# One run of key-value products per batch, and straight query pairs in the first two batches

## The chip, the cores and the metric

The kernel runs on one core of a Trainium2 chip. The metric is the device time of one execution in microseconds (us). Five engines work side by side, each in its own program order: TensorE multiplies matrices, VectorE does arithmetic between tensors, ScalarE functions and copies, GpSimd reductions over partitions, and SyncE issues the transfers (DMAs). Engines wait for each other by semaphores only.

## The reference

It is a linear attention, followed by a feed-forward layer with a gelu. For each of 8 batches and 8 heads (sequence 576, head size 64):

```
q_s = softmax of q over the 64 features
k_s = softmax of k over the 576 positions
kv  = k_s^T @ v               # 64 x 64 per head
x   = q_s @ kv                # 576 x 64 per head, heads side by side: 4608 x 512
h   = x @ w_in                # 512 x 2048
out = (h * sigmoid(1.702 h)) @ w_out
```

All is float32. The two weight matrices arrive as 64-bit floats and are turned into a high and a low 32-bit part in the kernel.

## The kernel before

**Tiles.** The 4608 tokens are 12 tiles (`t`) of 384, three to a partition. A batch is 576 tokens, one tile and a half: batch 0 starts at tile 0, batch 1 in tile 1, batches 2 to 7 in tiles 3, 4, 6, 7, 9, 10. Heads are taken in four pairs (`hp`). For a new batch, the keys' softmax numerators are made (`k_max`, `k_sub`: VectorE, GpSimd, and ScalarE for the exponential), then `kv_pair` (L435) multiplies keys by values: for each of a pair's two heads four full matmuls and one for the 64 positions left over ("tail"), with a column of ones in the values, whose product is the softmax's sum. TensorE runs each of these matmuls as two passes, so a pair shows as 20 in the trace, 64 columns wide, the two heads in two halves of the array. VectorE takes the reciprocal of the sum (L460, L461) and ScalarE scales the two 64x64 results into `kvn` (L466). Then queries are normalized (`q_soft`), transposed on TensorE (`q_tr`, L516) and multiplied with `kvn` (`x_pairs`): with one pair in a call as one 128x128 product whose off-blocks are zeros (L559), with two pairs as four 64x64 products that share the array (L564).

**Turned pairs.** For the four products of L564 to lie on different parts of the array, every second pair is held turned: its two heads change places, in the query's buffer (by the order of loading) and in `kvn`. This is done for all batches, though in tiles 0 and 1 the calls take one pair each.

**Feed-forward.** For each tile, 16 steps (`j`): `g1` (L589, 12 matmuls), gelu, and two steps later `g2` (L621, 9 matmuls). The first two tiles run interleaved, while the weights of the 16 steps are loaded (`load_w`, L218 and L223) and converted (`conv_w`: L248, L261 on ScalarE, L252, L256, L257, L267 on VectorE). The attention of a later tile is spread among the feed-forward steps of the tiles before it.

**Buffers and loads.** Batches 0 and 1 load all four heads of a group at once into memory that weights take over later. From batch 2 on keys and values go pair by pair through two buffers each (`kt_`, `vt_`): pairs 2 and 3 can be loaded only when the products of pairs 0 and 1 have read theirs. All loads are issued by SyncE, in one queue: `load_k` (L314, L319), `load_tail` (L298, L301), `load_v` (L330, one per head), `load_q` (L363 for tile 0, L368 else), with rows of 64 floats.

**Order.** A planner (`Plan`, L18) holds all operations with an engine, a cost, the buffers they read and write, and a rank, the due time. It runs a small model of the engines, always starting the ready operation of lowest rank, and the kernel's program on each engine is that order. So an operation's rank and cost say where it comes; on the chip the order is fixed. The rank of a task of tile t is `n0(i)`, i sixteenths of the way from three steps after the last step of tile t - 2 to the first step of tile t, 14 steps in all. Before, pairs 0 to 3 had their products at 4, 5.5, 10 and 11.5 and the query products of pairs 0 and 1 at 7.5, of pairs 2 and 3 at 13.5.

Of the kernel before, what the change touches and what calls it, by code (L numbers as in the profile page):

```python
# [107 lines left out]
def efficient_attention_then_gelu_ffn(  # L108
# [13 lines left out]
    nc = tc.nc  # L122
    B, H, S, D = q.shape
    NTOK, DM = out.shape
    FF = w_out.shape[0]
    P = 128
# [3 lines left out]
    NP = H // 2  # L130
# [4 lines left out]
    CM = SM // P  # L135
    ST = S - SM
    W = D + 1
# [4 lines left out]
    plan = Plan()  # L142

    bank = [psum.tile([P, 512], F32, name=f"bank{i}") for i in range(8)]

    def sb(name, shape, dtype=F32, tag=None):
        return const.tile(shape, dtype, name=name, tag=tag or name)

    ident = sb("ident", [P, P])
    kvn = [sb(f"kvn{i}", [P, NP, P]) for i in range(2)]  # L150
# [1 line left out]
    g = [sb(f"g{i}", [P, TB]) for i in range(3)]  # L152
    gs = [[sb(f"g{s}{i}", [P, TB], F32R) for s in "hl"] for i in range(LAG + 1)]
    tmp = [sb(f"tmp{i}", [P, DM]) for i in range(3)]
    kt_ = [sb(f"kt{i}", [P, CM, 2, D]) for i in range(2)]
    vt_ = [sb(f"vt{i}", [P, 2, CM, W]) for i in range(2)]
    qTs = [sb(f"qT{i}", [P, TB]) for i in range(2)]
    qt_ = [sb(f"qt{i}", [P, C, 2, D]) for i in range(2)]
    mx_ = [sb(f"mx{i}", [P, 4, D]) for i in range(2)]
# [26 lines left out]
    ek, em, ev, eq, en, etail = {}, {}, {}, {}, {}, {}  # L186
# [97 lines left out]
    def group(b):  # L284
        return 4 if b < 2 else 2

    kbuf, vbuf, qbuf, tbuf = {}, {}, {}, {}
# [17 lines left out]

    def load_k(b, i, rank):
        n = group(b)
        t, key = ek[b, i] if b < 2 else (kt_[i % 2], ("kt", i % 2))
        kbuf[b, i] = t, key
        hs = slice(n * i, n * (i + 1))  # L310

        def run():
            if b == 0:
                nc.sync.dma_start(  # L314
                    out=t.rearrange("p h c d -> p h (c d)"),
                    in_=k[b, hs, 0:SM, :].rearrange("h (p c) d -> p h (c d)", c=CM),
                )
            else:
                nc.sync.dma_start(out=t, in_=k[b, hs, 0:SM, :].rearrange("h (p c) d -> p c h d", c=CM))  # L319

        plan.add("SP", plan.ISSUE, (), (key,), rank, run, size=n * SM * D * 4)

    def load_v(b, i, rank):
        n = group(b)
        t, key = ev[b, i] if b < 2 else (vt_[i % 2], ("vt", i % 2))
        vbuf[b, i] = t, key

        def run():
            for h in range(n):
                nc.sync.dma_start(  # L330
                    out=t[:, h, :, 0:D], in_=v[b, n * i + h, 0:SM, :].rearrange("(p c) d -> p c d", c=CM)
                )

        plan.add("SP", n * 0.6, (), (key,), rank, run, size=1.5 * n * SM * D * 4)

    def parts(t):

        t0 = t * TB
        b, s0 = divmod(t0, S)
        n = min(TB, S - s0)  # L340
        got = [(b, s0, 0, n // C)]
        if n < TB:
            got.append((b + 1, 0, n // C, P))
        return got

    def load_q(t, i, rank):
        n = group(t)
        qt, key = eq[t, i] if t < 2 else (qt_[i % 2], ("qt", i % 2))
        qbuf[t, i] = qt, key

        if t == 0:
            runs = [(0, 0, 2), (2, 3, 1), (3, 2, 1)]
        elif n == 4:
            runs = [(0, 0, 1), (1, 1, 1), (2, 3, 1), (3, 2, 1)]
        else:
            runs = [(0, 1, 1), (1, 0, 1)] if i % 2 else [(0, 0, 2)]

        def run():
            for b, s0, p0, p1 in parts(t):
                for o, h, m in runs:  # L360
                    src = q[b, n * i + h : n * i + h + m, s0 : s0 + (p1 - p0) * C, :]
                    if t == 0:
                        nc.sync.dma_start(  # L363
                            out=qt[p0:p1, o : o + m].rearrange("p h c d -> p h (c d)"),
                            in_=src.rearrange("h (p c) d -> p h (c d)", c=C),
                        )
                    else:
                        nc.sync.dma_start(  # L368
                            out=qt[p0:p1, :, o : o + m], in_=src.rearrange("h (p c) d -> p c h d", c=C)
                        )  # L370

        plan.add("SP", plan.ISSUE * len(parts(t)) * len(runs), (), (key,), rank, run, size=n * TB * D * 4)
# [57 lines left out]
    def next_bank(t):  # L430

        n = nb[t] = nb.get(t, -1) + 1
        return n % 6 if t == 0 else 3 * (t % 2) + n % 3

    def kv_pair(b, hp, t, rank):  # L435
        n = group(b)
        i, o = divmod(2 * hp, n)
        kt, key = kbuf[b, i]
        vt, vkey = vbuf[b, i]
        kl, vl, (lkey, vlkey) = tbuf[b]  # L440
        bk = next_bank(t)
        pk = bank[bk]
        w = 2 * W
        hs = slice(2 * hp, 2 * hp + 2)
        loc = slice(o, o + 2)
        dst = kvn[b % 2][:, hp, :]
        r = rs[hp % 2]

        def run():
            for c in range(CM + 1):  # L450
                for a in range(2):
                    lhs = kt[:, c, o + a, :] if c < CM else kl[:, 2 * hp + a, :]
                    rhs = vt[:, o + a, c, :] if c < CM else vl[:, 2 * hp + a, :]
                    r0 = (a ^ hp % 2) * D
                    nc.tensor.matmul(  # L455
                        pk[r0 : r0 + D, :W], lhs, rhs, start=c == 0, stop=c == CM, tile_position=(0, r0)
                    )

        def run_r():
            nc.vector.tensor_scalar_add(r, pk[:, D:W], 1e-9)  # L460
            nc.vector.reciprocal(r, r)  # L461

        def run_n():
            for a in range(2):
                rows, cols = (slice(x * D, (x + 1) * D) for x in (a ^ hp % 2, a))
                nc.scalar.mul(dst[rows, cols], pk[rows, 0:D], r[rows])  # L466

        PB, R, K = ("bank", bk), ("r", hp % 2), ("kvn", b % 2, hp)
        plan.add("PE", 1.15, (key, vkey, lkey, (lkey, i), vlkey), (PB,), rank, run)
        plan.add("DVE", 0.35, (PB,), (R,), rank, run_r)  # L470
        plan.add("ACT", 0.65, (PB, R), (K,), rank, run_n)

    rs = [sb(f"r{i}", [P, 1]) for i in range(2)]
    qm = [sb(f"qm{i}", [P, C, 4]) for i in range(2)]

    def q_soft(t, i, ranks):
# [166 lines left out]
    def step_rank(t, j):  # L643
        if t == 0:
            return 2 * j
        if t == 1:
            return 2 * j + JOIN
        return 2 * NJ + JOIN + (t - 2) * NJ + j

    def new_batch(t):  # L650

        return next((b for b, s0, *_ in parts(t) if s0 == 0), None)
# [3 lines left out]
    def at(rank, f, *a):  # L656
        tasks.append((rank, len(tasks), f, a))


    for i in range(2):  # L660
        at(-90 + i, load_k, 0, i)
        if i == 0:
            at(-89.5, load_tail, 0)
    for i in range(2):
        at(-88 + i, load_q, 0, i)
    for i in range(2):
        at(-86 + i, load_v, 0, i)
    for j in range(NJ):
        r = -84 if j < 1 else -70 + j
# [12 lines left out]
    def attend(t, b, r, step):  # L682
        for i in range(2):
            at(r, k_max, b, i)
            at(r + step, k_sub, b, i)
            at(r + step, lambda rank, t=t, i=i: q_soft(t, i, (rank, rank, rank)))
            for hp in (2 * i, 2 * i + 1):
                at(r + 3 * step, lambda rank, hp=hp: kv_pair(b, hp, t, rank))
                at(r + 3 * step, q_tr, t, hp)
                at(r + 3.5 * step, x_pairs, t, (hp,))  # L690
            r += 2 * step
# [5 lines left out]
    for j in range(NJ):  # L697
        r = -40 if j == 0 else 2 * j - 2.2
# [3 lines left out]
    for t in range(2, NB):  # L702
        end = step_rank(t, 0)
        start = step_rank(t - 2, NJ - 1) + 3
        b = new_batch(t)

        def n0(i):
            return start + i * (end - start) / NJ + 0.3

        for gq in range(2):  # L710
            i0 = 6 * gq
            for hp in (2 * gq, 2 * gq + 1):
                d = (hp % 2) * 1.5

                ld = n0(5 + d) + 0.1 if gq else n0(0) - (7 if t == 2 else 3) + d
                if b is not None:
                    if hp == 0:
                        at(ld, load_tail, b)
                    at(ld, load_k, b, hp)
                    at(ld + 0.1, load_v, b, hp)  # L720
                    at(n0(i0 + d), k_max, b, hp)
                    at(n0(i0 + 1 + d), k_sub, b, hp)
                    at(n0(i0 + 4 + d), lambda rank, b=b, hp=hp, t=t: kv_pair(b, hp, t, rank))
                at(ld + 0.2, load_q, t, hp)
                at(n0(i0 + 1 + d), lambda rank, t=t, hp=hp: q_soft(t, hp, (rank, rank, rank)))
                at(n0(i0 + 5 + d), q_tr, t, hp)
                if hp % 2:
                    at(n0(i0 + 6 + d), x_pairs, t, (hp - 1, hp))
    seq = sorted((step_rank(t, j), t, j) for t in range(NB) for j in range(NJ))
    for n, (r, t, j) in enumerate(seq):  # L730
# [35 lines left out]
```

## Time and profile before

| | us |
|---|---|
| median of 3 runs | 924.39 (924.11 to 924.57) |
| the profiled execution, its own time | 925.09 |
| its span, first to last instruction | 923.3 |

| engine | busy us | share | instructions |
|---|---|---|---|
| TensorE (PE) | 885.3 | 96% | 5048 |
| TensorE weight loads (PEld) | 778.6 | 84% | 5048 |
| VectorE (DVE) | 392.7 | 43% | 863 |
| ScalarE (ACT) | 499.6 | 54% | 848 |
| GpSimd (POOL) | 24.0 | 3% | 35 |

The mean granted clock of TensorE over the span was 0.988 of full speed (2.4 GHz; its other level is 1.2 GHz). Matmuls are pipelined: a row's time is one matmul's latency, so what TensorE's work costs is read from start to start, not from the sum of durations. SyncE's rows (SPq) are the issuing of transfers, not their movement. A line number stands for the line of the kernel that made the instruction.

### The profile page before, as it was taken

Reading aid. Unit: us, or ns where it says so; the run is one execution under the profiler, and the core shown is the slowest. Engines: PE = TensorE matmul, PEld = TensorE weight load, DVE = VectorE, ACT = ScalarE, POOL = GpSimd, SP = SyncE. Lnnn points to the kernel's source line nnn. Section 1 sums busy time; section 2 is a strip of 40 time slices with the busy share of each in tenths; the row PEclk is TensorE's granted clock in tenths of the full one; section 3 lists DMA queues with packets and bytes.
Section 4 is the critical chain, followed back from the end, with each engine's and each line's share of the span. In section 5 each row is a group of like instructions: output and inputs, shape, how many; then the busy total and the mean of one; then the engine's idle time right before and its main releaser. Section 6 shows DMA issues by size and latency. Waiting matters only on the chain.

```text
span 923.3 us, 12812 instructions
## 1 busy us (share of the span) xinstructions
PE 885.3 (96%) x5048; PEld 778.6 (84%) x5048; DVE 392.7 (43%) x863; ACT 499.6 (54%) x848; POOL 24.0 (3%) x35
## 2 busy tenths in 40 slices
PE   2669999999999999999999999999999999999998
PEld 2469989888888889889889889889888888988996
DVE  8789995173342451331542442322344243131111
ACT  3476666367573783552773765544467375252322
POOL 1000000000000000000000000000000000000000
PEclk9879999999999999999999999999999999999999
DMA  9799100121221220001230230000231110000000
GB/s 224 173 377 278 26 1 1 51 75 40 51 58 33 57 50 35 18 18 40 58 75 35 64 75 35 18 18 35 63 65 45 36 37 9 35 18 1 35 1 34
DMA packets 124795, 55.35 MB, mean 60 GB/s; under 512 B 107840, under 2 KB 118080, under 8 KB 124736
## 3 DMA queue, kind: packets, MB, share of 16 engines
q1 hardware_dynamic: 124736, 54.54, 22.6%
q8 instruction: 39, 0.64, 0.3%
q14 instruction: 20, 0.16, 0.1%
HBM read 45.09 MB, written 9.44 MB: 59 GB/s over the span
## 4 chain that ended last, share of the span: by engine, by line
PE 93%; SPq 3%; DMA 1%; DVE 0%; ACT 0%; issue 0%; ACTq 0%
PE bank L589 44%; PE bank L621 44%; PE bank L455 2%; PE bank L564 2%; PE bank L516 2%; SPq L368 1%; SPq L330 1%; DMA raw<-in_moe_w_in 1%; DMA eq<-in_q 1%; SPq L298 0%; PE bank L559 0%; SPq L319 0%; SPq L301 0%; SPq L218 0%; SPq L314 0%
## 5 line engine op out<-in xcount | busy, mean ns | idle before, releaser
L589 PE MATMUL bank<-xh,w 128*128 128x384 f32 x1536 | 431.5, 342 | 7.4 <-ACT w L261 7.4
L621 PE MATMUL bank<-w,gh 128*128 128x512 f32 x1152 | 365.6, 399 | 1.4 <-ACT gh L598 1.4
L589 PEld LDWEIGHTS bank<-xh,w 128*128 128x128 f32 x1536 | 283.2, 189 | 18.8 <-ACT w L261 7.6
L601 DVE TENSOR_TENSOR gl<-g,gh 128x384 fp32r<-128x384 f32 x192 | 107.0, 557 | 398.4 <-ACT gh L598 398.0
L595 ACT ACTIVATE g<-bank 128x384 f32<-128x384 f32 x192 | 94.3, 491 | 309.8 <-PE bank L589 309.1
L589 PE MATMUL bank<-xl,w 128*128 128x384 f32 x768 | 260.5, 339 | 0.0
L621 PEld LDWEIGHTS bank<-w,gh 128*128 128x128 f32 x1152 | 211.9, 189 | 43.1 <-issue 6.2
L621 PE MATMUL bank<-w,gl 128*128 128x512 f32 x576 | 228.3, 396 | 3.1 <-DVE gl L601 3.1
L589 PEld LDWEIGHTS bank<-xl,w 128*128 128x128 f32 x768 | 145.5, 189 | 6.5
L621 PEld LDWEIGHTS bank<-w,gl 128*128 128x128 f32 x576 | 108.7, 189 | 28.6 <-DVE gl L601 3.5
L598 ACT CAST gh<-g 128x384 fp32r<-128x384 f32 x192 | 98.6, 513 | 5.8
L595 ACT ACT_TABLE_LOAD x58 | 74.4, 1283 | 1.0
L489 DVE TENSOR_REDUCE qm<-qt 128x6 f32<-128x384 f32 x40 | 21.9, 548 | 51.4 <-DMA qt<-in_q 51.4
L493 ACT ACT_TABLE_LOAD x33 | 42.3, 1283 | 2.4 <-DMA qt<-in_q 1.8
L397 POOL PARTITION_ALL_REDUCE mx<-mx x28 | 22.9, 817 | 717.1 <-DVE mx L393 717.1
L523 ACT COPY qT<-bank 128x384 f32<-128x384 f32 x48 | 22.7, 475 | 26.6 <-PE bank L516 26.4
L466 ACT ACTIVATE kvn<-bank,r 64x64 f32<-64x64 f32 x64 | 19.7, 308 | 25.2 <-DVE r L461 23.1
L421 ACT ACT_TABLE_LOAD x25 | 32.1, 1283 | 1.2 <-PEq L753 0.7
L496 DVE TENSOR_REDUCE qm<-qt 128x6 f32<-128x384 f32 x40 | 22.0, 550 | 20.5 <-ACT qt L493 20.5
L248 ACT ACTIVATE tmp<-raw 128x512 f32<-128x512 f32 x32 | 21.5, 676 | 16.4 <-DMA raw<-in_moe_w_in 9.4
L534 DVE TENSOR_TENSOR xl<-bank,xh 128x384 fp32r<-128x384 f32 x48 | 24.7, 551 | 3.5 <-ACT xh L531 3.3
L490 DVE TENSOR_TENSOR qt<-qt,qm 128x384 f32<-128x384 f32 x40 | 22.3, 559 | 3.3
(72 smaller groups left out, 464.6 us busy)
## 6 DMA issues: line engine op xcount, KB each, us to landing
out<-tmp SPq DMA_DIRECT2D x36, 256.0 KB, 2.1
raw<-in_moe_w_in SPq DMA_DIRECT2D x16, 512.0 KB, 10.0
raw<-in_moe_w_out SPq DMA_DIRECT2D x16, 512.0 KB, 10.5
kt<-in_k SPq DMA_DIRECT2D x24, 256.0 KB, 3.5
vt<-in_v SPq DMA_DIRECT2D x48, 128.0 KB, 3.5
qt<-in_q SPq DMA_DIRECT2D x40, 96.0 KB, 2.8
qt<-in_q SPq DMA_DIRECT2D x14, 192.0 KB, 3.0
ek<-in_k SPq DMA_DIRECT2D x4, 512.0 KB, 6.4
```

Source lines behind the costliest of these rows:

```text
L397: nc.gpsimd.partition_all_reduce(flat, flat, P, bass_isa.ReduceOp.max)
L421: nc.scalar.activation(t, t, AF.Exp)
L490: nc.vector.tensor_tensor(out=qt, in0=qt, in1=bc(m, D), op=ALU.subtract)
L493: nc.scalar.activation(qt, qt, AF.Exp)
L496: nc.vector.tensor_reduce(out=m, in_=qt, axis=AX.X, op=ALU.add)
L523: nc.scalar.copy(qT, pq[:, :TB])
L534: nc.vector.tensor_tensor(out=xl, in0=px[:, :TB], in1=xh.bitcast(F32), op=ALU.subtract)
L589: nc.tensor.matmul(ph, wi[w][j][:, c, :], x[:, c, :], start=c == 0 and i == 0, stop=c == KC - 1 and i == 2,)
L595: nc.scalar.activation(gt, ph, AF.Gelu_apprx_sigmoid)
L598: nc.scalar.copy(gh, gt)
L601: nc.vector.tensor_tensor(out=gl, in0=gt, in1=gh.bitcast(F32), op=ALU.subtract)
L621: nc.tensor.matmul(po[c], x[:, cs], wo[w][j], start=j == 0 and i == 0, stop=j == NJ - 1 and i == 2)
```

## The change

It makes four edits. Keys and values get four buffers each in place of two, and a batch's four loads of each are asked for together before the tile's tasks. `kv_pairs` takes a list of pairs: from batch 2 on all four in one uninterrupted run on TensorE, into four stretches of one PSUM bank, due at 6.5; one addition and one reciprocal serve all four, and the eight scalings of ScalarE follow. In batches 0 and 1 it is called with one pair, as before. Pairs are turned only from batch 2 on, so the queries of tiles 0 to 2 are loaded straight, all heads of a group in one transfer per part; tile 2 (which belongs to batch 1) then calls `x_pairs` with single pairs. The planner's cost of the products goes from 1.15 a pair to 0.57 a pair and 0.36 a run, and that of the early query loads falls with the number of transfers.

```
-    kt_ = [sb(f"kt{i}", [P, CM, 2, D]) for i in range(2)]
-    vt_ = [sb(f"vt{i}", [P, 2, CM, W]) for i in range(2)]
+    kt_ = [sb(f"kt{i}", [P, CM, 2, D]) for i in range(NP)]
+    vt_ = [sb(f"vt{i}", [P, 2, CM, W]) for i in range(NP)]
...
+    def turned(b, hp):
+        return b > 1 and hp % 2 == 1
...
     def load_q(t, i, rank):
-        if t == 0:
-            runs = [(0, 0, 2), (2, 3, 1), (3, 2, 1)]
-        elif n == 4:
-            runs = [(0, 0, 1), (1, 1, 1), (2, 3, 1), (3, 2, 1)]
-        else:
-            runs = [(0, 1, 1), (1, 0, 1)] if i % 2 else [(0, 0, 2)]
+        runs = [(0, 1, 1), (1, 0, 1)] if turned(parts(t)[0][0], i) else [(0, 0, n)]
...
-    def kv_pair(b, hp, t, rank):
+    def kv_pairs(b, hps, t, rank):
...
+        pk = bank[bk][:, : len(hps) * W].rearrange("p (m w) -> p m w", w=W)
+        nr[0] += 1
+        r = rs[nr[0] % 2][:, : len(hps)]
...
         def run():
-            for c in range(CM + 1):
+            for m, hp in enumerate(hps):
+                i, o = divmod(2 * hp, n)
+                kt, vt = kbuf[b, i][0], vbuf[b, i][0]
+                for c in range(CM + 1):
+                    for a in range(2):
+                        lhs = kt[:, c, o + a, :] if c < CM else kl[:, 2 * hp + a, :]
+                        rhs = vt[:, o + a, c, :] if c < CM else vl[:, 2 * hp + a, :]
+                        r0 = (a ^ turned(b, hp)) * D
+                        nc.tensor.matmul(
+                            pk[r0 : r0 + D, m, :], lhs, rhs, start=c == 0, stop=c == CM, tile_position=(0, r0)
+                        )
...
+            nc.vector.tensor_scalar_add(r, pk[:, :, D], 1e-9)
+            nc.vector.reciprocal(r, r)
...
+        plan.add("PE", 0.57 * len(hps) + 0.36, reads, (PB,), rank, run)
+        plan.add("DVE", 0.35, (PB,), (R,), rank, run_r)
...
+                    nc.scalar.mul(kvn[b % 2][rows, hp, cols], pk[rows, m, 0:D], r[rows, m : m + 1])
...
-                    at(ld, load_k, b, hp)
-                    at(ld + 0.1, load_v, b, hp)
-                    at(n0(i0 + d), k_max, b, hp)
-                    at(n0(i0 + 1 + d), k_sub, b, hp)
-                    at(n0(i0 + 4 + d), lambda rank, b=b, hp=hp, t=t: kv_pair(b, hp, t, rank))
+                    lk = n0(0) - (7 if t == 2 else 3) + hp
+                    at(lk, load_k, b, hp)
+                    at(lk + 0.1, load_v, b, hp)
+                    at(n0(hp), k_max, b, hp)
+                    at(n0(hp + 1), k_sub, b, hp)
+                    if hp == NP - 1:
+                        at(n0(6.5), lambda rank, b=b, t=t: kv_pairs(b, range(NP), t, rank))
...
-                if hp % 2:
+                if t == 2:
+                    at(n0(i0 + 6 + d), x_pairs, t, (hp,))
+                elif hp % 2:
                     at(n0(i0 + 6 + d), x_pairs, t, (hp - 1, hp))
```

## Rows read from the trace of the kernel before

**Rows 1.** The page's line of engines: busy us (share of the span) x instructions.
```profile
PE 885.3 (96%) x5048; PEld 778.6 (84%) x5048; DVE 392.7 (43%) x863; ACT 499.6 (54%) x848; POOL 24.0 (3%) x35
```
**Rows 2.** Windows; PE, PEld, DVE, ACT, POOL busy; last: clock, DMA share, GB/s.
```profile
150.00:912.00 762.00, 762.00 (x4351) 670.46 (x4350) 261.03 (x608) 406.25 (x681) 16.83 (x23) 1.00 0.16 39
...
20.00:40.00 20.00, 14.85 (x95) 10.27 (x95) 18.45 (x35) 13.26 (x26) 2.12 (x2) 0.87 0.73 126
40.00:60.00 20.00, 9.52 (x78) 8.51 (x75) 12.09 (x24) 11.48 (x22) 0.00 (x0) 0.71 1.03 359
60.00:80.00 20.00, 19.09 (x110) 17.63 (x111) 18.30 (x36) 13.01 (x29) 0.00 (x0) 0.91 1.02 330
```
**Rows 3.** The chain that ended last, 0 to 90 us: start, us, what.
```profile
40.22 8.07 DMA raw<-in_moe_w_in
...
49.55 4.30 PE bank L589 x12
...
69.70 2.09 PE bank L589 x12
71.79 2.08 PE bank L621 x9
```
**Rows 4.** Timeline of SyncE, 0 to 110 us: start, us, issues merged by line.
```profile
3.34 3.26 SPq L363 DMA_DIRECT2D eq<-in_q  x6
...
20.15 13.45 SPq L368 DMA_DIRECT2D eq<-in_q  x16
33.65 5.32 SPq L330 DMA_DIRECT2D ev<-in_v  x8
39.01 0.62 SPq L218 DMA_DIRECT2D raw<-in_moe_w_in  x1
```
**Rows 5.** Windows of 2 us in the opening, columns as in rows 2.
```profile
24.00:26.00 2.00, 2.00 (x26) 1.28 (x26) 1.57 (x3) 1.93 (x6) 0.00 (x0) 1.00 1.14 168
...
28.00:30.00 2.00, 2.00 (x11) 1.69 (x11) 1.97 (x5) 1.35 (x4) 0.00 (x0) 1.00 0.35 80
```
**Rows 6.** The page's DMA issues: KB each, median us from issue to landing.
```profile
ev<-in_v SPq DMA_DIRECT2D x16, 128.0 KB, 3.3
...
eq<-in_q SPq DMA_DIRECT2D x16, 48.0 KB, 2.4
```
**Rows 7.** Timelines of VectorE and of ScalarE in the opening; idle before in brackets.
```profile
38.93 0.96 DVE L499 TENSOR_TENSOR eq<-eq,qm 128x768 f32<-128x768 f32 x1
45.54 0.43 DVE L252 TENSOR_SCALAR raw<-raw 128x512 uint32<-128x512 uint32 x1 [5.66 <-DMA raw<-in_moe_w_in]
...
54.52 0.48 ACT L523 COPY qT<-bank 128x384 f32<-128x384 f32 x1 [1.70 <-PE bank L516]
```
**Rows 8.** Line L455 from 150 us on: idle of its engine (us, times).
```profile
  issue: 6.2, 22
```
**Rows 9.** Timeline of TensorE around the first insertion of the third batch.
```profile
200.32 0.34 PE L589 MATMUL bank<-xh,w 128*128 128x384 f32 x1
200.59 0.69 PE L455 MATMUL bank<-vt,kt 128*64 128x65 f32 x16
201.10 0.29 PE L455 MATMUL bank<-vl,kl 128*64 128x65 f32 x4
...
201.60 0.33 PE L589 MATMUL bank<-xl,w 128*128 128x384 f32 x1
```
**Rows 10.** Instructions on the raw weights: ns min/median/max, first and last start us.
```profile
L248 ACT ACTIVATE tmp<-raw x32: 647/677/697, 17.9 to 133.4; 128x512 f32<-128x512 f32 x32
```
**Rows 11.** Timeline of TensorE: a paired insertion, then an unpaired one of tile 1.
```profile
182.95 0.34 PE L589 MATMUL bank<-xh,w 128*128 128x384 f32 x1
...
184.59 0.40 PE L621 MATMUL bank<-w,gl 128*128 128x512 f32 x1
...
67.28 0.39 PE L621 MATMUL bank<-w,gl 128*128 128x512 f32 x1
...
68.61 0.39 PE L621 MATMUL bank<-w,gl 128*128 128x512 f32 x1
```
**Rows 12.** The page's group of the scalings: busy, mean ns of one, idle before.
```profile
L466 ACT ACTIVATE kvn<-bank,r 64x64 f32<-64x64 f32 x64 | 19.7, 308 | 25.2 <-DVE r L461 23.1
```

More of the change, by code (lines that the diff above doesn't have):

```diff
@@ L307, in load_k @@
         n = group(b)
-        t, key = ek[b, i] if b < 2 else (kt_[i % 2], ("kt", i % 2))
+        t, key = ek[b, i] if b < 2 else (kt_[i], ("kt", i))
         kbuf[b, i] = t, key
@@ L324, in load_v @@
         n = group(b)
-        t, key = ev[b, i] if b < 2 else (vt_[i % 2], ("vt", i % 2))
+        t, key = ev[b, i] if b < 2 else (vt_[i], ("vt", i))
         vbuf[b, i] = t, key
@@ L363, in run @@
                         nc.sync.dma_start(
-                            out=qt[p0:p1, o : o + m].rearrange("p h c d -> p h (c d)"),
+                            out=qt[p0:p1].rearrange("p h c d -> p h (c d)"),
                             in_=src.rearrange("h (p c) d -> p h (c d)", c=C),
@@ L433, in next_bank @@
         return n % 6 if t == 0 else 3 * (t % 2) + n % 3
-    def kv_pair(b, hp, t, rank):
+    def kv_pairs(b, hps, t, rank):
         n = group(b)
-        i, o = divmod(2 * hp, n)
-        kt, key = kbuf[b, i]
-        vt, vkey = vbuf[b, i]
         kl, vl, (lkey, vlkey) = tbuf[b]
         bk = next_bank(t)
[L442 to L447, printed above, removed]
-        def run():
-            for c in range(CM + 1):
-                for a in range(2):
[L452 to L471, printed above, removed]
@@ L473, in efficient_attention_then_gelu_ffn @@
-    rs = [sb(f"r{i}", [P, 1]) for i in range(2)]
+        pk = bank[bk][:, : len(hps) * W].rearrange("p (m w) -> p m w", w=W)
+        nr[0] += 1
+        r = rs[nr[0] % 2][:, : len(hps)]
+        reads = [lkey, vlkey]
+        for hp in hps:
+            i = 2 * hp // n
+            reads += [kbuf[b, i][1], vbuf[b, i][1], (lkey, i)]
+        def run():
+            for m, hp in enumerate(hps):
[9 more added lines that the diff above has]
+                        )
@@ new lines, in run_r, with run_n @@
+        def run_r():
+            nc.vector.tensor_scalar_add(r, pk[:, :, D], 1e-9)
+            nc.vector.reciprocal(r, r)
+        PB, R = ("bank", bk), ("r", nr[0] % 2)
+        plan.add("PE", 0.57 * len(hps) + 0.36, reads, (PB,), rank, run)
+        plan.add("DVE", 0.35, (PB,), (R,), rank, run_r)
+        for m, hp in enumerate(hps):
+            def run_n(m=m, hp=hp):
+                for a in range(2):
+                    rows, cols = (slice(x * D, (x + 1) * D) for x in (a ^ turned(b, hp), a))
+                    nc.scalar.mul(kvn[b % 2][rows, hp, cols], pk[rows, m, 0:D], r[rows, m : m + 1])
+            plan.add("ACT", 0.65, (PB, R), (("kvn", b % 2, hp),), rank, run_n)
@@ L474, in efficient_attention_then_gelu_ffn @@
+    nr = [0]
+    rs = [sb(f"r{i}", [P, NP]) for i in range(2)]
     qm = [sb(f"qm{i}", [P, C, 4]) for i in range(2)]
@@ L687, in attend @@
             for hp in (2 * i, 2 * i + 1):
-                at(r + 3 * step, lambda rank, hp=hp: kv_pair(b, hp, t, rank))
+                at(r + 3 * step, lambda rank, hp=hp: kv_pairs(b, (hp,), t, rank))
                 at(r + 3 * step, q_tr, t, hp)
```

## The prediction

> **What bounds the kernel now.** The views, in the order of reading. The page's engine line first: TensorE is busy for 885.3 of 923.3 us [rows 1], so the reader looks for where it is not, and for what its busy time is spent on. The windows answer the first: from 150 to 912 us it is busy without a gap at the full 2.4 GHz, while from 20 to 40 us it is busy for 14.85 us and from 40 to 60 us for 9.52, at a mean granted clock of 0.71 [rows 2]. So there are two places to win: its own work in the long middle, and the opening. From 60 to 80 us it is busy for 19.09, with its last gap just after 60; a start of this dense part that comes n us earlier ends the kernel n us earlier, as long as the others keep up.
>
> The chain of waits tells what ends the opening's largest gap. It runs through a weight load issued at 40.22 that lands 8.07 us later, ScalarE's work on it, and the first product of the step at 49.55 [rows 3]. Going back, it is SyncE's own issuing: the sixteen query loads of the second token tile take SyncE 13.45 us from 20.15, the eight value loads behind them 5.32, and only then come the weights [rows 4]. Between 28 and 30 us the DMA engines are busy to 0.35 and move 80 GB/s, where between 24 and 26 they were full (1.14 at 168 GB/s) [rows 5]: past 26 us issuing is the limit, not moving.
>
> **Part 1, the query loads of the first two tiles.** Unturned, a group's four heads go in one transfer. The second tile's 16 issues become 4. SyncE's 13.45 us hold 16 issues, so one is at most 0.84; without the stall at their head it is about 0.65 (the eight value issues behind: 5.32/8 = 0.67) [rows 4]. Twelve fewer are 12 x 0.65 = 7.8 us, the most that the weights can move up. The first tile's 6 issues become 2, worth 4 x 0.54 = 2.2 us of 3.26 [rows 4], which I put at nothing: the DMA engines are full then and hide it (with that cover gone it would be 2.2 us more).
>
> The bytes do not shrink, so the engines bound it from below. At 26 us, where the engines first run dry, (26 - 20.15 - 3.05 of stall)/0.65, some 4 of the 16 query loads of 48 KB [rows 6] are through; 12 x 48 + 8 x 128 KB = 1.6 MB are left ahead of the weights. At 168 GB/s, the full rate of [rows 5], this takes 9.5 us and ends at 35.5; at 80/0.35 = 229 GB/s, 7.0 us and 33.0. Before, the last values were issued at about 38.3 and land 3.3 us later [rows 6], at 41.6. So the weights come 6.1 us earlier at least, and 7.8 at most (SyncE's own saving). A rule of the Trainium skill speaks for the lower end (DMA: Bandwidth & Descriptors, "Why small descriptors are slow"): each packet carries a fixed overhead whatever the issue, and 256-byte packets feel it. By it the bytes would go at the slower rate and the weights gain 6.1 us; the row of 0.35 shows that before, at least, the packets were not the limit.
>
> What is late next? VectorE: its last operation before the gap starts at 38.93 and takes 0.96, so it is free at 39.9, and it then stood idle 5.66 us until 45.54 for the weights [rows 7]. Weights that land 6.1 us earlier or more close this gap whole: 5.7 us, the lower end for the opening. TensorE's product could start near 43.5. The upper end is the clock. TensorE idles 7.39 us before 49.55 and its product then takes 4.30 us, against 2.09 at the full clock [rows 3]; ScalarE waits 1.70 us for TensorE at 54.52 because of it [rows 7]. With a gap of one or two us in place of 7.39 the clock may stay up, which gives up to 1.7 us more: 7.4. I take 6.8, since the gap almost vanishes. Behind it the weights' order is kept, and VectorE and TensorE move up together. (If VectorE moved up less than TensorE, TensorE would wait for it: that is the lower end, 5.7.)
>
> **Part 2, four products in one run.** From the third batch on (six batches), four separate insertions among the feed-forward products become one. There are 24 now, and 22 of them show an idle weight loader without any wait, 0.28 us each [rows 8]. One insertion in full [rows 9]: from the last ordinary start, 200.32, to the second ordinary start behind it, 201.60, are 1.28 us, where two ordinary spacings of 2.09/12 = 0.174 would be 0.35; it costs 0.93. The first sixteen of its 20 matmuls take 0.51 us from start to start, 0.032 each, so 20 carry 0.64, and 0.29 is spent going in and out. Three times less of that in six batches: 18 x 0.29 = 5.2 us. This is the lower end (the last four may start closer than the others; were they free, 0.42 would be in and out, 7.6 us). I take 0.30: 5.4 us. All of it is on the path, as TensorE is never idle there. The reciprocals drop from 4 to 1 pair of instructions a batch, on VectorE, which has slack: nothing. The keys and values of a batch are now requested together, two more of each kind at once; SyncE and the DMA engines (0.16 busy in the middle [rows 2]) hide that. At the start they stand before the last weights in SyncE's queue: 1 MB more, 4.5 to 6.0 us by the rates of part 1, hidden as long as they land before their conversions, the last of which starts at 133.4 [rows 10]. The two more fills of ones on VectorE lie in its idle start: nothing.
>
> **Part 3, the third tile's query products.** They lose the paired form: two insertions of four 64x64 products become four of one 128x128. Paired, an insertion costs 184.59 - 182.95 = 1.64, less one spacing of 0.17 and two of 2.08/9 = 0.23 [rows 3]: 1.01 us for two pairs. The second tile's unpaired form, two halves of 192 columns, costs 68.61 - 67.28 = 1.33, less three of 0.23: 0.64 for one pair [rows 11]. With 384 columns in one piece it has two passes in place of four, so at most 0.64 and at least two spacings and a way out, about 0.46. Four of these less two of the other: -0.2 to +0.5; I take +0.3. The Trainium skill (TensorEngine Tiling (Array Packing), "Theoretical Speedup") would have it dearer: work cut to 64x64 tiles may run up to four times faster, so untiling it should cost. By that rule, half the array now multiplies zeros and the time would double, +2.0 us; no row shows that.
>
> **Sum.** -6.8 - 5.4 + 0.3 = -11.9 us against the profiled execution's own 925.09 gives 913.2. That execution is 0.7 above the median of the three runs, 924.39; the prediction for the median is 912.5. A measurement of this kernel can tell about 0.2%, 1.85 us, from no change. Ends: -7.4 - 7.6 - 0.2 and -5.7 - 5.2 + 0.5 give 909.2 and 914.0.
>
> **Rivals.**
> Rival 1: the opening gains little, because the DMA engines stay full on small packets once they are issued faster, or VectorE takes its freed time for other work. Then only parts 2 and 3 count: 924.4 - 5.4 + 0.3 = 919.3, and with half the gain 915.9. Against it: busy shares of 0.35 in the stretch that matters [rows 5] and VectorE's 5.66 us of idleness for nothing but weights [rows 7].
> Rival 2: the merged run is followed too closely by its readers, and this ends slower. The first query products read the scaled results of ScalarE: eight scalings of 308 ns [rows 12] come now after the whole run, 2.5 us, where one pair's 0.6 did. The tasks stand 14/16 of a step apart, 0.875 x (2.09 + 2.08) = 3.6 us. If ScalarE is so late by its tables and gelus that all 2.5 us are waited for, six batches lose 15 us: 927.5. It decides from 2.0 us a batch, where the gain is gone. Against it: the order is made from costs of all engines, and today's has no wait of TensorE from 150 to 912 us [rows 2].
> Rival 3: the unpaired form streams its zeros at full price, so that the 1.01 us of each paired insertion doubles; part 3 then costs 2.0 us and not 0.3: 914.2. The second tile's 0.64 for a pair in the same form [rows 11] speaks against. (It is what the Trainium skill's page in part 3 would lead to.)
> Rival 4: the merged run gains nothing since its inner pairs pay the same way in and out: 917.9. Against: the in and out of [rows 9] lie between matmuls of different forms, and inside the run the form stays.
>
> **How the numbers follow.** Forecast 0.70 (909.2 to 914.0); rival 1 0.13, half of it below 917; rival 2 0.04; rival 3 0.06; rival 4 0.04; an order that the new costs shuffle, either way, 0.03. The range 908.5 to 917.0 holds the forecast, rival 3 and half of rival 1. Faster takes all but rival 2 and part of the shuffle: 0.94; same 0.02; slower 0.04.
>
> **What would show it.** Right: SyncE issues the first of the later weights near 31 us and not 39.01; VectorE has no gap of some 5 us near 40; the product of 49.55 starts near 43 and takes about 2.1 us; TensorE has six runs of 80 matmuls of about 2.85 us in place of 24 of 0.93; no waits behind them. Wrong: a DMA share near 1 from 26 us on with the weights still landing after 43 (rival 1), or TensorE waiting for the scalings behind a run (rival 2).

## The result, and the profile after

The median went from 924.28 us (924.11 to 924.57, four runs) to 915.93 (914.18 to 918.02, four runs): a ratio of 0.991, 95% interval 0.9884 to 0.9936, faster by 8.35 us. The forecast was 912.5 with a range of 908.5 to 917.0; its likeliest case alone reached to 914.0. The profiled execution took 914.53 us for a span of 912.8, where before's took 925.09 for 923.3.

Of the page of after, the line of engines and the group of the scalings (columns as in [rows 1] and [rows 12]):

```profile
PE 880.8 (96%) x5040; PEld 778.0 (85%) x5040; DVE 388.8 (43%) x829; ACT 494.1 (54%) x844; POOL 25.1 (3%) x35
...
L472 ACT ACTIVATE kvn<-bank,r 64x64 f32<-64x64 f32 x64 | 17.9, 306 | 14.1 <-DVE r L462 12.2
```

TensorE is again the bound. The scalings on ScalarE cost 306 ns each as before and wait for the reciprocals, but from 60 us on TensorE's products wait for nothing.

The windows of the opening (columns as in [rows 2]):

```profile
20.00:40.00 20.00, 14.63 (x98) 10.03 (x98) 18.32 (x36) 14.77 (x27) 2.13 (x2) 0.83 1.06 231
40.00:60.00 20.00, 14.60 (x126) 12.59 (x123) 18.65 (x38) 15.16 (x31) 0.00 (x0) 0.91 1.06 384
60.00:80.00 20.00, 19.89 (x100) 17.59 (x99) 19.35 (x35) 14.03 (x27) 0.00 (x0) 1.00 0.88 254
...
24.00:26.00 2.00, 1.94 (x28) 1.41 (x27) 1.93 (x6) 1.79 (x5) 0.00 (x0) 1.00 1.37 177
28.00:30.00 2.00, 2.00 (x11) 1.70 (x11) 1.97 (x5) 1.52 (x3) 0.00 (x0) 1.00 0.80 128
```

From 40 to 60 us TensorE is busy for 14.60 us, where it was 9.52, at a mean granted clock of 0.91 in place of 0.71 [rows 2]. From 28 to 30 us the DMA engines are busy to 0.80, where it was 0.35 [rows 5].

SyncE's timeline, then VectorE's and TensorE's where each begins on the second step (columns as in [rows 4] and [rows 7]):

```profile
3.33 1.35 SPq L362 DMA_DIRECT2D eq<-in_q  x2
4.72 7.81 SPq L330 DMA_DIRECT2D ev<-in_v  x8
...
19.90 4.93 SPq L367 DMA_DIRECT2D eq<-in_q  x4
24.88 7.37 SPq L330 DMA_DIRECT2D ev<-in_v  x8
32.29 0.62 SPq L218 DMA_DIRECT2D raw<-in_moe_w_in  x1
```

```profile
38.67 0.96 DVE L503 TENSOR_TENSOR eq<-eq,qm 128x768 f32<-128x768 f32 x1
39.55 0.42 DVE L252 TENSOR_SCALAR raw<-raw 128x512 uint32<-128x512 uint32 x1
```

```profile
42.95 0.44 PE L593 MATMUL bank<-xh,w 128*128 128x384 f32 x1 [1.65 <-ACT w L261]
```

The weights are issued at 32.29 in place of 39.01 [rows 4]. VectorE turns from the queries to the weights without a gap, where it stood idle 5.66 us [rows 7]. TensorE begins the step at 42.95 in place of 49.55 [rows 3], after 1.65 us of idleness and not 7.39.

TensorE around the run of the third batch (columns as in [rows 9]):

```profile
216.89 0.34 PE L593 MATMUL bank<-xh,w 128*128 128x384 f32 x1
217.06 0.49 PE L520 MATMUL bank<-ident,qt 128*128 128x128 f32 x3
217.48 0.69 PE L456 MATMUL bank<-vt,kt 128*64 128x65 f32 x16
218.00 0.29 PE L456 MATMUL bank<-vl,kl 128*64 128x65 f32 x4
218.11 0.64 PE L456 MATMUL bank<-vt,kt 128*64 128x65 f32 x16
218.58 0.29 PE L456 MATMUL bank<-vl,kl 128*64 128x65 f32 x4
218.70 0.64 PE L456 MATMUL bank<-vt,kt 128*64 128x65 f32 x16
...
219.75 0.29 PE L456 MATMUL bank<-vl,kl 128*64 128x65 f32 x4
219.97 0.74 PE L625 MATMUL bank<-w,gh 128*128 128x512 f32 x2
220.54 0.40 PE L625 MATMUL bank<-w,gl 128*128 128x512 f32 x1
```

The last ordinary start is 216.89, the second behind the run is one spacing of 0.23 before 220.54, at 220.31: 3.42 us, less spacings of 0.17 and 0.23, is 3.01. The three transposes of a query tile, which stand in the same gap, cost 0.33 in such a gap alone. The run costs 2.69 us, against 4 x 0.93 [rows 9], and there are six: 6 x 1.03 = 6.2 us saved. The view of the line's idle time from 150 us on counts the ways in, 22 before [rows 8]:

```profile
  issue: 1.0, 6
```

The third tile's query products, two pairs one behind the other (same view as the run):

```profile
175.32 0.33 PE L593 MATMUL bank<-xh,w 128*128 128x384 f32 x1
175.50 1.45 PE L563 MATMUL bank<-qT,kvn 128*128 128x384 f32 x4
176.49 0.92 PE L625 MATMUL bank<-w,gh 128*128 128x512 f32 x2
177.25 0.39 PE L625 MATMUL bank<-w,gl 128*128 128x512 f32 x1
```

Worked in the same way these two pairs cost 1.28 us, the other two, which stand behind transposes, 1.48: together 2.76, where the paired form took 2 x 1.01 [rows 11]. The loss is 0.75 us.

**Where the time went.** A step that no part but the opening touches yet starts at 172.04 us before and at 164.32 after: the opening gives 7.7. From there to the end before takes 751.3 us and after 748.5, only 2.8 less, where the run (6.2) less the third tile (0.75) should give 5.4. So 2.6 us are lost somewhere in the middle, in which TensorE's products never wait. The ordinary products show it: counted over all steps that nothing interrupts, twelve products of the first weights take 2104 ns from start to start before and 2109.5 after, three of the second weights 695.3 and 698.6.

### The profile page after: what moved, and what is told of

It is laid out like the page before. It is cut to its first block, busy times and chain, and to the rows that moved or that the text cites. A ratio compares the mean times of both kernels' runs of the same rounds, so it can differ in the third digit from the quotient of the medians.

```text
span 912.8 us, 12680 instructions
## 1 busy us (share of the span) xinstructions
PE 880.8 (96%) x5040; PEld 778.0 (85%) x5040; DVE 388.8 (43%) x829; ACT 494.1 (54%) x844; POOL 25.1 (3%) x35
## 4 chain that ended last, share of the span: by engine, by line
PE 94%; DVE 4%; ACT 1%; DMA 1%; issue 0%; SPq 0%; ACTq 0%; DVEq 0%
PE bank L593 44%; PE bank L625 44%; PE bank L456 2%; PE bank L520 2%; PE bank L568 2%; PE bank L563 1%; DMA ek<-in_k 1%; DVE eq L494 0%; DVE tmp L257 0%; DVE tmp L256 0%; DVE qm L493 0%; DVE qm L500 0%; DVE w L267 0%; DVE em L414 0%; DVE xl L538 0%
```

## The experiments

**Is it the chip, and do the parts add up?** Four kernels on one chip, five rounds each; before and after again, and each part by itself. The before of this chip is 925.16.

> The kernel before once more, on the chip of the three runs below. Theory A (the ordinary feed-forward products became slower by the change: three g2 products took 695 ns from start to start in the trace of before and 698.6 in that of after, twelve g1 products 2103 and 2109): the same 695 and 2103 here. Rival B (that difference is one of chips or of days): 698 to 699 and 2109 here, and the time of before about 3 us longer than 924.3.

> The changed kernel once more, with more runs. Its four runs lay at 914.2 to 914.5 and at 917.3 to 918.0. Theory: two courses of the opening, told apart by how long TensorE's clock is at half (10.2 us in the trace at hand, one stretch of 3.4 us more in the longer runs), so the runs fall into the same two groups and the trace shows the group of its own time. Rival: a spread without groups, from the transfers. Theory A: g2 products at 698.6 ns again. Rival B: whatever the kernel before shows on this chip.

e1 gave 924.68 (ratio 0.9997, 0.9989 to 1.0006), e2 916.59 (0.9902, 0.9887 to 0.9918). The ordinary products of e1 take 695.4 and 2103.5 ns, those of e2 698.6 and 2109.5: the slower pace goes with the kernel, not with the chip.

The query loads and the third tile alone, with two buffers and four separate products a batch:

```
+    def turned(b, hp):
+        return b > 1 and hp % 2 == 1
-        if t == 0:
-            runs = [(0, 0, 2), (2, 3, 1), (3, 2, 1)]
...
+        runs = [(0, 1, 1), (1, 0, 1)] if turned(parts(t)[0][0], i) else [(0, 0, n)]
...
-                    r0 = (a ^ hp % 2) * D
+                    r0 = (a ^ turned(b, hp)) * D
...
+                if t == 2:
+                    at(n0(i0 + 6 + d), x_pairs, t, (hp,))
```

> The straight query pairs of batches 0 and 1 alone, with separate products and two buffers. Additive theory: the opening's 7.5 us less and the third tile's 0.8 more, so 917.6; TensorE's product of the second step starts at 43 and not at 49.5. Rival: the opening needs the earlier keys as well, and less than 4 us come: over 920. If the slower ordinary products come from the larger buffers, they are at 695 ns here.

920.4 us, ratio 0.995 (0.9936 to 0.9963). Products at 695.3 and 2104 ns: two buffers, the old pace. The third tile costs 0.8, as expected, and TensorE's product of the second step starts at 42.80. Yet the same untouched step starts only 4.8 us earlier than in e1, where 7.5 were expected: the time missed 917.6 by 2.8 us and lies where the rival put it. The granted clock is at half for 17.1 us of this trace's opening, and for 10.2 of after's. Whether this is the cause is open, for one of the five runs had a mean granted clock of 0.994, where the others had 0.990, and took 920.4 like them. That the opening's full gain needs the earlier keys as well isn't ruled out by this run alone.

The run and its four buffers alone, on after:

```
-        return b > 1 and hp % 2 == 1
+        return hp % 2 == 1
...
-        runs = [(0, 1, 1), (1, 0, 1)] if turned(parts(t)[0][0], i) else [(0, 0, n)]
+        if t == 0:
+            runs = [(0, 0, 2), (2, 3, 1), (3, 2, 1)]
...
-                if t == 2:
-                    at(n0(i0 + 6 + d), x_pairs, t, (hp,))
-                elif hp % 2:
+                if hp % 2:
```

> One run of four products and four buffers alone, all batches turned as before, 16 and 6 early query loads. Additive theory: six runs of 2.7 us where there were 24 of 0.93, 6.2 us less: 918.1, and if it is the larger buffers that slow the ordinary products, about 921 with 698.6 ns. The opening is that of before: the product of the second step at 49.5.

920.58 us, ratio 0.995 (0.9938 to 0.9963), with products at 698.6 and 2109.5 ns, as expected. The two parts alone give 4.8 and 4.6 us against 925.16, 9.3 together, and e2 gave 8.6: they add up within their intervals, and the slower pace comes with the part that has the four buffers.

**Is it what the buffers do, or where they put the rest?** With four buffers of each kind everything behind them in memory lies 8,256 bytes further on in each partition, the weights with it. This kernel is before, with the two extra buffers of each kind laid out and never loaded; short fills of the extra buffers are added at its start, and its order of work is before's otherwise.

```
-    kt_ = [sb(f"kt{i}", [P, CM, 2, D]) for i in range(2)]
-    vt_ = [sb(f"vt{i}", [P, 2, CM, W]) for i in range(2)]
+    kt_ = [sb(f"kt{i}", [P, CM, 2, D]) for i in range(NP)]
+    vt_ = [sb(f"vt{i}", [P, 2, CM, W]) for i in range(NP)]
...
+    for t in kt_[2:]:
+        nc.vector.memset(t[:, 0], 0.0)
```

> The kernel before, with its program's order and its 24 separate products, but with four buffers of each kind laid out (two are never loaded), so that all that lies behind them, the weights too, is 8256 bytes further on in each partition, as in the changed kernel. Theory A1 (the place of the weights in memory sets the pace of the feed-forward products): a third of a g2 step 698 to 699 ns and a g1 step 2109 where before has 695 and 2103; 2.5 to 3 us longer than before. Rival A2 (the order of work on TensorE sets it): 695 and 2103, and the time of before.

926.92 us against 924.87, ratio 1.0027 (1.0018 to 1.0036): slower, by 2.05 us, a little less than expected. TensorE's timeline, the starts of one step and of a later one; e1 first, then e5:

```profile
180.15 0.42 PE L589 MATMUL bank<-xh,w 128*128 128x384 f32 x1
...
909.69 0.34 PE L589 MATMUL bank<-xh,w 128*128 128x384 f32 x1
```

```profile
179.01 0.42 PE L591 MATMUL bank<-xh,w 128*128 128x384 f32 x1
...
910.69 0.34 PE L591 MATMUL bank<-xh,w 128*128 128x384 f32 x1
```

The same products in the same order take 729.54 us in e1 and 731.68 in e5, with 698.6 and 2110 ns for the ordinary ones in e5. The two ran on different chips, but before and this kernel were timed on one, and e3 and e7 (below) have the old pace on either. The place in memory alone does it.

**Can it be given back?** After, with a pad of 64 or of 960 bytes in each partition behind the buffers (the code is that of 64; the other has `[P, 240]`). With 960 the weights lie 9,216 bytes behind their places in before, at the same remainder by 1,024.

```
+    pad = sb("pad", [P, 16])
...
+    nc.vector.memset(pad[:, 0:1], 0.0)
```

> The changed kernel with 64 more bytes between the new buffers and what lies behind, so that the weights start at the same remainders of 128 bytes as in the kernel before. Theory A1, if remainders of 128 matter: 695 and 2103 ns, 2.5 to 3 us less than the changed kernel, about 913.5. A1, if larger distances matter: some other pace. Rival A2: 698.5 and 2109 ns, the changed kernel's time.

> As the run before, with 960 bytes: the same remainders of 1024 bytes as in the kernel before. Theory A1: 695 and 2103 ns, also if 128 bytes are not enough. Rival A2: 698.5 and 2109 ns.

e6 gave 912.85 us (ratio 0.9872, 0.9857 to 0.9888) and e7 913.12 (0.9879, 0.9865 to 0.9893), against 0.991 and 0.9902 for after in its two measurements. The starts of one step and of a later one again, in after, e6 and e7:

```profile
173.33 0.42 PE L593 MATMUL bank<-xh,w 128*128 128x384 f32 x1
...
900.01 0.34 PE L593 MATMUL bank<-xh,w 128*128 128x384 f32 x1
```

```profile
173.26 0.42 PE L595 MATMUL bank<-xh,w 128*128 128x384 f32 x1
...
896.75 0.34 PE L595 MATMUL bank<-xh,w 128*128 128x384 f32 x1
```

```profile
175.20 0.42 PE L595 MATMUL bank<-xh,w 128*128 128x384 f32 x1
...
898.90 0.34 PE L595 MATMUL bank<-xh,w 128*128 128x384 f32 x1
```

726.68 us in after, 723.49 and 723.70 in the padded ones: about 3 us come back with both. They do so in different ways: e7's products have before's pace (695.0 and 2104 ns), in e6 the first weights' are faster than in any kernel before it (2091) and the second weights' as slow as in after (698.8). The expectation for e6, 695 and 2103, was wrong in both, though its time came within 0.7 us.

**Was it issuing?** After with the query loads of the first tiles cut up by head again, in the straight order:

```
-        runs = [(0, 1, 1), (1, 0, 1)] if turned(parts(t)[0][0], i) else [(0, 0, n)]
+        runs = [(0, 1, 1), (1, 0, 1)] if turned(parts(t)[0][0], i) else [(h, h, 1) for h in range(n)]
```

> The changed kernel, straight pairs as there, but the early queries loaded head by head: 8 issues for the first tile and 16 for the second in place of 2 and 4, with the same bytes and packets. Theory (issuing is what held the weights back): the first of the later weights is issued near 40 us and not near 32, the product of the second step starts near 49 and not 43, and 5 to 7 us of the gain are gone: about 922. Rival (the packets hold it back, or the order of heads did): near 32 to 34 us, the changed kernel's time of 916.5.

922.52 us, ratio 0.9975 (0.9964 to 0.9986). SyncE's timeline of this kernel:

```profile
22.53 13.12 SPq L367 DMA_DIRECT2D eq<-in_q  x16
35.70 5.32 SPq L330 DMA_DIRECT2D ev<-in_v  x8
41.06 0.62 SPq L218 DMA_DIRECT2D raw<-in_moe_w_in  x1
```

The same bytes in sixteen transfers take SyncE 13.12 us again, the weights are issued at 41.06, and TensorE's second step begins at 49.8. Of the 8.6 us that e2 gained on its chip, 2.35 are left: the opening's gain came from fewer issues.

**Does the gain of a run lie in its ends?** On e6 (64 bytes), with two runs of two pairs a batch:

```
-    at(n0(6.5), lambda rank, b=b, t=t: kv_pairs(b, range(NP), t, rank))
+    at(n0(6.5), lambda rank, b=b, t=t: kv_pairs(b, (0, 1), t, rank))
+    at(n0(8.5), lambda rank, b=b, t=t: kv_pairs(b, (2, 3), t, rank))
```

> The padded kernel (64 bytes), with the products of a batch in two runs of two pairs, due at 6.5 and 8.5, in place of one run of four. Theory (a run costs a fixed way in and out and the same for each pair: from 0.93 us for one pair and 2.69 for four follow 0.345 and 0.585): a run of two takes 1.52 us, six runs more cost 6 x 0.345 = 2.1 us, about 914.9. Rival (pairs inside a run pay again, and the gain came from elsewhere): 912.9 as with one run.

915.18 us, ratio 0.9902 (0.9886 to 0.9917); e6 taken again on the same chip (e11 below) gave 913.72. TensorE around the first of the two runs:

```profile
218.94 0.34 PE L595 MATMUL bank<-xh,w 128*128 128x384 f32 x1
219.11 0.49 PE L522 MATMUL bank<-ident,qt 128*128 128x128 f32 x3
219.53 0.69 PE L458 MATMUL bank<-vt,kt 128*64 128x65 f32 x16
220.05 0.29 PE L458 MATMUL bank<-vl,kl 128*64 128x65 f32 x4
...
220.85 0.73 PE L627 MATMUL bank<-w,gh 128*128 128x512 f32 x2
221.42 0.40 PE L627 MATMUL bank<-w,gl 128*128 128x512 f32 x1
```

A run of two costs 2.25 - 0.17 - 0.23 - 0.33 = 1.52 us, beside 0.93 for one pair and 2.69 for four. That is a line: 0.58 to 0.59 for each pair and 0.34 for going in and out. Six more runs cost 6 x 0.34 = 2.1 us by it; the stretch from 204 us to the last step is 2.0 longer than in e11, the medians stand 1.5 apart.

**Both weights in good places.** On e6, with all the later-loaded first weights laid out together, a gap of 128 bytes, and then the second weights, so that the first lie at a remainder of 64 by 256 bytes and the second at 192:

```
+    for kind in ("wi", "wo"):
+        for j in range(NJ):
+            if f"{kind}{j}" not in held:
+                sb("place", [P, 2 * DM], tag=f"{kind}{j}")
+        if kind == "wi":
+            gap = sb("gap", [P, 32])
```

> The padded kernel again, with the places of the weights chosen by the pace that the traces show for each remainder of 256 bytes: w_in's stay at 64, where a g1 matmul takes 172.8 ns, and w_out's (seven of sixteen; the others lie in the early buffers) go from 64 to 192, where a g2 matmul took 230.5 to 231.5 ns and not 233.5. Theory A1: 7 steps x 9 matmuls x 12 tiles x 2 to 3 ns = 1.5 to 2.3 us less than the 64-byte padding, about 911. Rival (the pace hangs on something else that the layouts had in common): no difference, 912.9.

> The padded kernel (64 bytes) once more, on the chip of the two runs above, for comparison: 912.9, and g1 matmuls at 172.8 ns where the weights lie at 64.

e10: 911.22 us (908.79 to 912.07), where about 911 was expected, ratio 0.9853 (0.9836 to 0.9869). e11: 913.72 (912.81 to 914.52), ratio 0.9884 (0.987 to 0.9897). In e10 both products have the fast pace, 694.7 and 2090 ns:

```profile
175.34 0.42 PE L601 MATMUL bank<-xh,w 128*128 128x384 f32 x1
...
896.74 0.34 PE L601 MATMUL bank<-xh,w 128*128 128x384 f32 x1
```

This is 721.40 us for the stretch that takes 726.68 in after and 723.50 in e11. It is the best version found: the change, with the weights' places chosen, 13.2 us under the before of its chip (924.42).

## Why the prediction was right, and where it was off

The direction, the parts and their order of size were as forecast. The number came out 3.4 us low, and outside the likeliest case's own range. By steps:

- **Part 1, -6.8, with ends at -5.7 and -7.4.** The mechanism held. The weights were issued 6.7 us earlier, between the bounds of 6.1 and 7.8, VectorE's gap closed, and e8 shows that the number of issues was the cause. The first tile's saving was indeed given back: its issues take 1.35 us in place of 3.26 [rows 4], but the value loads behind them 7.81, where before they took 5.95, and the second tile's queries start only 0.25 earlier. A row bears on why the weights were issued only 6.7 us earlier and not 7.8: from 24 to 30 us the DMA engines are now busy at 0.80 and more. The bound of 6.1 was worked out for the landing of the last values. Here are the last two value loads, with the time from issue to landing, before and then after:

```profile
L330 SPq DMA_DIRECT2D ev<-in_v x2: 628/628/629, 37.7 to 38.3; - x2
DMA to landing us min/median/max: 3.2/3.3/3.3
```

```profile
L330 SPq DMA_DIRECT2D ev<-in_v x2: 628/630/631, 30.9 to 31.6; - x2
DMA to landing us min/median/max: 3.3/3.6/4.0
```

  The last value load lands at 41.6 before and at 35.6 after: about 6 us earlier, and the sum at the slower rate had 35.5. The first weights land 6.5 us after their issue at 39.01 before and 5.5 us after 32.29 now, so they come 7.7 us earlier. The Trainium skill (DMA: Bandwidth & Descriptors, "Why small descriptors are slow (HBM only)") says that each small packet carries a fixed overhead; the prediction took the slower rate to be what follows from it, and the values' landing agrees with that rate. That the packets are the reason is not shown: no run here changes their size.
- **The size of part 1 was put down as one number, and it is two.** In the profiled run the opening gave 7.7 us against before's profiled run, over the upper end; in e2 the same step starts at 166.38, which is 5.7 against that run, the lower end, and 4.9 against e1, whose own opening was 0.8 shorter. The step that failed is "I take 6.8, since the gap almost vanishes", and the upper end, which counts the clock for one product alone (1.7 us): TensorE's granted clock has two courses after the change. From 42 to 52 us it is 1.00 in after's profiled run and 0.83 in that of e2, here in this order:

```profile
42.00:52.00 10.00, 5.35 (x43) 4.26 (x43) 9.63 (x21) 9.29 (x19) 0.00 (x0) 1.00 1.06 383
```

```profile
42.00:52.00 10.00, 7.08 (x46) 5.80 (x44) 8.31 (x19) 7.89 (x17) 0.00 (x0) 0.83 1.07 390
```

  The 0.83 is a mean over times at 2.4 and at 1.2 GHz. After 30 us the clock is at half for 20.5 us in all before, for 10.2 in after's trace and for 13.65 in e2's, as e2's expectation said. The nine runs of the changed kernel fall in two groups by the mean granted clock of the whole run: 0.994 in the four that took 914.18 to 914.78, 0.993 in the five that took 916.59 to 918.28. That the course seen in the two traces lies behind the other seven runs too is likely, and not shown; what sets the course stays open.
- **Part 2, -5.4, with ends at -5.2 and -7.6.** Measured: -6.2. The ways in and out are 0.34 us and not the 0.30 that was taken, because the matmuls start closer than the 0.032 taken for each: the last four of a pair take 0.11 (218.00 to 218.11), 0.028 each, as the second end allowed, and the sixteen of an inner pair 0.47 (218.11 to 218.58), where the first pair's take 0.52. e9 confirms it with runs of another length, and so rules out rival 4 (inner pairs pay the same).
- **Part 3, +0.3, with ends at -0.2 and +0.5.** Measured: +0.75. The step that failed is the price of a pair, "at most 0.64 and at least two spacings and a way out, about 0.46": a pair cost 0.64 in the first insertion and 0.74 in the second. A pass of 384 columns of these products takes 0.32 us from start to start in the first and 0.32 to 0.43 in the second, about twice the 0.175 of an ordinary product of the same size. The trace of before had this: the second tile's passes of only 192 columns already start 0.16 apart, about an ordinary spacing, so two passes in place of four of half the width save nothing. The Trainium skill (TensorEngine Tiling (Array Packing), "Theoretical Speedup") gives up to twice for each dimension of 64 or less, so up to four times for 64x64 tiles is an estimate from it; the prediction worked its rival out to twice the price, +2.0. Here the paired form was worth 2.76/2.02 = 1.4 times, so rival 3 (twice the price) was too dear and the forecast too cheap.
- **Four buffers, put at nothing.** This is the term that was missing. The extra loads and fills cost nothing, as said; that a buffer moves everything behind it was not in the sum. It costs 3.0 us in after (726.68 less the 723.70 of e7, where before's places by remainder are restored), and 2.05 in e5 on its own.
- **The sum again.** With what was measured, -7.7 - 6.2 + 0.75 + 3.0 = -10.15 for the profiled run, whose span fell by 10.5; 0.4 is not accounted for. Without the 3.0 the forecast of the median would have been good: e6 and e7, which have the change and give the pace back, take 912.85 and 913.12. That closeness is partly luck: part 2 came 0.8 better and part 3 0.45 worse than said, and the opening lies on either side of its 6.8.
- **Rivals 1 and 2.** Rival 1 (the opening gains little) fell with the 32.29 us at which the weights are issued. Rival 2 (the merged run is followed too closely) isn't seen. From 60 us on the list of waits of after (us in total, times, longest) has this for the query products and the scalings:

```profile
PEld bank L568 <- ACT kvn L472: 1.1, 3, 0.4
```

  It is the weight loader alone, three times and 1.1 us in all, and the products have no wait: the eight scalings' 2.5 us are hidden between a run and its readers. The paired query insertions cost the same 1.01 us as before.

## What to carry to other kernels

Where one engine issues all loads, count issues in the opening: sixteen transfers merged into four had the loads behind them issued 6.7 us earlier, although not a byte less was moved. Small products that need another form of the array are worth gathering in one run, since each visit costs the same 0.34 us whatever its length. And after any change that adds or resizes a buffer, compare the pace of the untouched products with before's, from start to start: a loss that no wait and no idle time shows may be the place of their operands, and a pad of 64 bytes tries it out.

## What the runs showed of the hardware

The pace of back-to-back products depended on where their weights lie in memory. The later-loaded weights can be sorted by the remainder of their place in a partition by 256 bytes; within a kernel all the later-loaded weights of a kind have the same. The first weights' products (the weights are the loaded operand) take 172.9 to 173.6 ns from start to start at a remainder of 64, in all eight buffers, and 175.6 to 176.0 at 0, in all eight; at 192 five of the eight take 176.3 to 176.7, and the other three lie between 173.0 and 176.7. For the second weights (the streamed operand, 512 columns) the order is another: 233.6 to 233.7 ns at 64 and 232.4 to 232.7 at 0, in all seven, and 228.9 to 231.0 at 192. At 0 and 64 each step repeats its value within 1 ns in all tiles; some of the three at 192 change from tile to tile. The pace does not follow the chip: 695.3 and 2104 ns in e3 and 695.0 and 2104 in e7, which ran on two. What lies behind this was not found, the remainder alone does not settle it, and the runs show it for these products of 128x128 weights alone.

The clock's course in the opening differed between runs of one kernel, and was worth about 2 us of the end: the same untouched step starts at 164.32 in after's profiled run and at 166.38 in e2's, with 10.2 and 13.65 us at half clock before it.
